# RWKV-7 attention with a hardswish feed-forward: the load of unit 4's r moved behind the second group's preparation, and the second inversion's steps moved behind a stage's results

## The chip, the cores and the metric

The kernel runs on one core of one Trainium2 chip. The metric is the device time of one execution in microseconds (us), the median of several; less is better. Nothing else runs on the chip.

## The reference, cut to what matters

All data are float32. The first half is a recurrence over 768 time steps for 4 batches of 8 heads, each with a 40x40 state; the second is a two-layer feed-forward on its output.

```python
B, H, S, D = 4, 8, 768, 40
for t in range(S):
    y[:, :, t] = einsum('bhd,bhde->bhe', r_t, state)
    Sa = einsum('bhde,bhe->bhd', state, a_t)
    state = state * w_t[:, :, None, :] - einsum('bhd,bhe->bhde', Sa, b_t)
    state = state + einsum('bhd,bhe->bhde', v_t, k_t)
x = y.transpose(0, 2, 1, 3).reshape(3072, 320)
h = x @ w_in                                   # 320 -> 2048
out = (h * clip(h + 3, 0, 6) / 6) @ w_out      # 2048 -> 320
```

## The kernel before, in words

**Units and groups.** Time is cut into blocks of 64 steps. A *unit* is two batches by one such block; there are 24. Four units form a *group* (two blocks of time by two pairs of batches); unit 4 to unit 7 are the second group. Within a block the recurrence is written as matrix products, which need the inverse of a triangular matrix per head.

**Preparation of a unit** (function `prepare`, L582) is a list of stages. Most have two halves: *products* on PE into PSUM, a `yield PE`, and then *results*, which ACT, DVE or POOL take out of PSUM. The stages are W and gam (the decays), A, B, K (PE transposes of the loaded a, b, k at L506, then a product with the decays on DVE: L650, L658, L736), F (the triangular matrix: L672 on PE, L676 on ACT), factor (PE L710, ACT `rgt` L717, then POOL makes the scaled k and b, `KBt`, L725), E (scores at L554 on PE, then the mask, `copy_predicated` L578, on DVE) and EV (PE L752, ACT L757). A stage also issues the loads of a later unit that reuse the buffers it has just read (`fetch`, L490 for w, a, b, k; L487 for v; L478 for r and for a of later units).

**Inversion** (function `invert`, L779) takes the F of a whole group: a transpose on DVE (L784), a copy on ACT (L794), cuts and memsets on POOL (L789, L791, L796), then 30 pairs of a product (L804) and a sum (L810) on DVE, and two transposes at the end (L813, L818). It is a generator. Each call `aside(n)` issues its next n steps; the first step issues everything up to L796, the next two issue nothing, and then each step is one DVE instruction.

**Feed-forward.** `feed_forward` is a generator too; `pieces(n)` issues its next n pieces: 8 matmuls of expand (L1171; results on ACT L1193 and DVE L1194) or 2 or 4 of contract (L1219).

**Order.** Every engine runs its instructions in program order, so the order in which these generators are advanced is the order on each engine. SP issues nearly all DMAs, in program order as well. While the first group's last stages run by a written plan (loop at L1416, lines t = 10 to 15 of it), `by_twos` (L1309) prepares units 4 to 7 beside them: in its line t it runs one stage of units 4 and 5 (t below 9) and one of units 6 and 7 (t = 3 and t above 5), with feed-forward pieces after each. Units 6 and 7 have their F stage in line 10, after which the second inversion is put on the list `side`; lines 11, 12 and 13 are their factor, E and EV stages. What is left of `second_group` is run at L1446, then 18 times three steps and 1.25 pieces (L1448), then the rest of the inversion.

Then the main loop begins with unit 4's own steps: `begun_beside` clears buffers on POOL (L567, L570), `fade` scales the state (L911, L913), and `RT` turns r on DVE (L531). That is the first use of unit 4's r.

The two places that the change touches, L1323 to L1324 and L1431 to L1434:

```python
                    run(chains[i], steps if t > 10 else 0, mixed, 1 if t < 5 else 0)
                pieces(rate / 2)
...
        if t == BEGIN + 2:
            fetch("V", NU)
            fetch("V", NU + 1)
            fetch("R", NU)
```

`run(stage, steps, ...)` calls `aside(steps)` at each `yield PE`, so between a stage's products and its results. `mixed` is 0 in the only call.

Of the kernel before, what the change touches and what calls it, by code (L numbers as in the profile page):

```python
# [31 lines left out]
def kernel(  # L32
# [47 lines left out]
    NU = 2 * NP  # L80
# [30 lines left out]
    def begun_ffn():  # L111

        lent.__exit__(None, None, None)
        pairs.clear()
        pairs.append(("pair", 2))
        pools["h"] = ctx.enter_context(tc.tile_pool(name="hidden", bufs=1, space=PSUM))
# [77 lines left out]
    def second(name):  # L194

        tag = {"B": "S", "K": "U"}[name]
        return padded(grp.tile([P, H, SLOT], F32, name=name + "1", tag=tag, bufs=1), name)

    def seconds():
        t = inv.tile([P, 2, H, SLOT], F32, name="WA1", tag="x", bufs=1)  # L200
        for i, name in enumerate("WA"):
            others[name] = padded(t[:, i], name)
# [28 lines left out]
    for i in range(3):  # L231
        t = area[:, EDGE + i * H * BL:EDGE + (i + 1) * H * BL]
# [14 lines left out]
    for p in range(NP):  # L247
        t = const.tile([P, 2, NPR, SLOT], F32, name=f"state{p}")
        nc.vector.memset(t[:], 0.0)
        state.append(t)  # L250
        t = const.tile([P, 2, NPR], F32, name=f"last{p}")
# [16 lines left out]
    for i, (x, y) in enumerate([(0, DFF // 2), (0, NJ // 2)]):  # L268
        for n, z in enumerate((x, y)):
            t = win[:, :, z:z + H * SLOT] if i == 0 else \  # L270
                wout[:, z:z + 4, :].rearrange("p j m -> p (j m)")[:, 0:2 * H * SLOT].rearrange(
                    "p (n x) -> p n x", n=2)
            t = t.rearrange("p n (h e) -> p n h e", e=SLOT)
# [4 lines left out]
    for u in range(2):  # L278
        t = win2[:, u * NPR * P:(u + 1) * NPR * P]
# [171 lines left out]
    def fetch(name, i, engine=None):  # L451

        if i is None or i >= NK:
            return
        x, crossed = {"W": (w, 0), "A": (a, 0), "B": (b, 0), "K": (k, 0), "R": (r, 1),
                      "V": (v, 1)}[name]
        if name == "V":
            t = values[i % AHEAD]
        else:
            t = placed.get((name, i))  # L460
            if (name, i) == ("R", 1):
                t = others["K"]
            if (name, i) == ("W", NU + 1):
                t = values[NU]
            t = t if t is not None else (others if i < 2 * NU and i % 2 and name != "R" else inputs)[name]
        g, p = names[i]
        engines = engine or nc.sync
        if name == "R" and i >= NU or name == "A" and i >= 2 * NU:
            y = x[2 * p:2 * p + 2, :, g * BL:(g + 1) * BL, :]
            n = 2 if name == "R" else 1  # L470
            y = y.rearrange("q (k s j) t e -> s j (q k) (t e)", s=2, j=n).rearrange(
                "s j k (l e) -> s j l k e", e=2 * D)
            for s in range(2):
                for c in range(0, D, L):
                    z = s * SLOT + c
                    to = rooms[name][z:z + L].rearrange("l (j k e) -> l j k e", j=n, e=2 * D)
                    for j in range(n):
                        nc.sync.dma_start(out=to[:, j, :, 0:2 * D - c], in_=y[s, j, :, :, c:])  # L478
            data[i][name + "N"] = t
            return  # L480
        for q in range(2):
            engine = engines[q] if isinstance(engines, tuple) else engines
            y = x[2 * p + q, :, g * BL:(g + 1) * BL, :]
            rows = slice(q * BL, (q + 1) * BL)
            if crossed:
                for s in range(2):
                    engine.dma_start(out=t[rows, 4 * s:4 * s + 4, 0:D],  # L487
                                     in_=y[s::2].rearrange("h t e -> t h e"))
            else:
                engine.dma_start(out=t[rows, :, 0:D], in_=y.rearrange("h t e -> t h e"))  # L490
        data[i][name + "N"] = t
# [272 lines left out]
    def in_turn(stages, order):  # L764

        for name in order:
            yield from stages[name]()
            shared[0] = None
            yield DONE

    def by_stages(i, stages):


        scanned = [] if i < NU + 2 else ["W", "gam"]
        order = ["K", "factor", "F"] if i % NU < 2 else ["K", "F", "factor"]
        return in_turn(stages, scanned + ["A", "B"] + order + ["E", "EV"])
# [476 lines left out]
    def pieces(n):  # L1253

        owed[0] += n * (8 / 9 if spread[0] else 1)
        while owed[0] >= 1:
            owed[0] -= 1
            if not next(stream):
                owed[0] = 0.0

    def aside(n, weight=0):

        for _ in range(n):
            if side and next(side[0], side) is side:
                side.popleft()
            due[0] += weight
            while due[0] >= 1:
                due[0] -= 1
                next(weights, None)

    def deal(n):

        for _ in range(n):
            next(weights, None)

    def run(stage, steps=0, mixed=0, deals=0):

        for at in stage:
            if at == DONE:
                return  # L1280
            aside(steps, mixed)
            deal(deals)
# [13 lines left out]
    def prepared(i):  # L1296
        nonlocal F
        if i >= NK:
            return None
        if i % NU == 0:  # L1300
            F = lazy_F()
        return prepare(i, F)
# [6 lines left out]
    def by_twos(first, steps, mixed, rate):  # L1309


        chains = [by_stages(first + i, prepared(first + i)) for i in range(NU)]
        for t in range(TWOS):

            order = [0, 1] if t < STAGES else []
            order += [2, 3] if t > 5 else []
            if t < 2:
                order = [0, 1, 0, 1][4 * t:]
            if t == 3:
                order = [2, 0, 3, 1]  # L1320
            for i in order:
                if t >= 2 or first != NU:
                    run(chains[i], steps if t > 10 else 0, mixed, 1 if t < 5 else 0)  # L1323
                pieces(rate / 2)  # L1324
            if t == 10:
                side.append(invert(group_F[-1], third, first == 0))
            yield
# [12 lines left out]
    chains = [in_turn(begin[i], [x[1:] for x in FIRST + BESIDE if x[0] == str(i)]) for i in range(NU)]  # L1340
# [17 lines left out]
    chains = [in_turn(stages[0], ["RT", "VT", "C", "R"]), in_turn(stages[1], ["RT", "VT", "C"])]  # L1358
# [25 lines left out]
    def block(i, j):  # L1384

        if i % NU < 2:
            if j == 0:
# [24 lines left out]
    chains = {str(i): in_turn(stages[i], [x[0][1:] for line in plan for x in line if x[0][0] == str(i)])  # L1412
              for i in range(NU)}
    chains.update({x: firsts[n] for n, x in enumerate("XY")})
    chains.update({x: in_turn(prepare(NU + n, None), ["W", "gam"]) for n, x in enumerate("PQ")})
    for t, line in enumerate(plan):  # L1416
        if t == 8:
            begun_ffn()
            ring.clear()
            ring.extend([("one", 1), ("whole", 2)])  # L1420
        for name, *amounts in line:
            run(chains[name[0]], 0, 0, *map(int, amounts))
        limit[0] = {3: 15, 8: 17, 9: PIECES}.get(t, limit[0])
        if t == BEGIN - 2:
            seconds()
            third.clear()
            second_group = by_twos(NU, 3, 0, 1.25)
        if t == BEGIN:
            fetch("A", NU + 1)
            fetch("W", NU + 3)  # L1430
        if t == BEGIN + 2:  # L1431
            fetch("V", NU)
            fetch("V", NU + 1)
            fetch("R", NU)  # L1434
        if t == BEGIN + 1:

            for name in "BK":
                others[name] = second(name)
                fetch(name, NU + 1)
        if t >= BEGIN - 2:  # L1440
            pieces(3 if t < BEGIN else 1.5 if t < BEGIN + 3 else 0)
        if t >= BEGIN:
            next(second_group)
    for _ in weights:
        pass
    for _ in second_group:  # L1446
        pass
    for _ in range(18):  # L1448
        aside(3)
        pieces(1.25)  # L1450
# [154 lines left out]
```

## Time and profile before

| what | value |
|---|---|
| median of three timed runs | 775.2 us (773.38 to 775.27) |
| the profiled execution | 772.7 us |
| its span, first to last instruction | 771.0 us (1.7 us lie around it) |
| PE, TensorE matmul, busy | 710.8 us (92%) |
| DVE, VectorE, busy | 508.8 us (66%) |
| ACT, ScalarE, busy | 310.4 us (40%) |
| POOL, GpSimd, busy | 150.8 us (20%) |
| mean granted TensorE clock | 0.956 |

In timelines a row reads: start in us from the beginning of the span, length in us, engine, line of the code, operation, what it writes and reads, shape, count; a bracket gives how long the engine was idle before it and what ended the wait. SPq is the queue of SP, where a row is the time that the issue of DMAs took. PEld is the load of a matmul's stationary operand, and PEclk the share of full clock granted to TensorE.

### The profile page before, as it was taken

Reading aid. Unit: us, or ns where it says so; the run is one execution under the profiler, and the core shown is the slowest. Engines: PE = TensorE matmul, PEld = TensorE weight load, DVE = VectorE, ACT = ScalarE, POOL = GpSimd, SP = SyncE. Lnnn points to the kernel's source line nnn. Section 1 sums busy time; section 2 is a strip of 40 time slices with the busy share of each in tenths; the row PEclk is TensorE's granted clock in tenths of the full one; section 3 lists DMA queues with packets and bytes.
Section 4 is the critical chain, followed back from the end, with each engine's and each line's share of the span. In section 5 each row is a group of like instructions: output and inputs, shape, how many; then the busy total and the mean of one; then the engine's idle time right before and its main releaser. Section 6 shows DMA issues by size and latency. Waiting matters only on the chain.

```text
span 771.0 us, 33034 instructions
## 1 busy us (share of the span) xinstructions
PE 710.8 (92%) x14568; PEld 603.1 (78%) x14568; DVE 508.8 (66%) x1027; ACT 310.4 (40%) x644; POOL 150.8 (20%) x303
## 2 busy tenths in 40 slices
PE   4635888999899989999999999999999999999997
PEld 3534777778779778888888888888888888888885
DVE  8899968588557799556798456898436982333210
ACT  2377865232553324552434453234444224322211
POOL 7403210321322211212112121203112010000000
PEclk7956799999999999999999999999999999999999
DMA  9685563420334322233322223313331110110000
GB/s 124 119 179 150 114 170 57 79 43 18 64 65 84 70 55 48 52 71 60 64 52 55 53 62 63 69 37 60 57 72 42 25 24 23 35 35 12 14 16 19
DMA packets 175999, 48.43 MB, mean 63 GB/s; under 512 B 159216, under 2 KB 174576, under 8 KB 175856
## 3 DMA queue, kind: packets, MB, share of 16 engines
q1 hardware_dynamic: 171552, 45.58, 29.7%
q8 instruction: 115, 1.88, 1.0%
q10 hardware_dynamic: 4304, 0.74, 0.7%
q14 instruction: 28, 0.23, 0.1%
HBM read 37.62 MB, written 3.93 MB: 54 GB/s over the span
## 4 chain that ended last, share of the span: by engine, by line
PE 77%; DVE 8%; SPq 5%; issue 3%; DMA 3%; ACT 3%; POOL 0%; DVEq 0%; ACTq 0%; POOLq 0%
PE o L1219 25%; PE h L1171 24%; PE pair L554 4%; PE pair L1064 4%; SPq L490 3%; PE h L1184 2%; PE one L506 2%; PE pair L968 2%; PE pair L927 1%; DVE prod L804 1%; PE pair L1007 1%; PE pair L516 1%; PE pair L752 1%; DVE x L810 1%; PE pair L1023 1%
## 5 line engine op out<-in xcount | busy, mean ns | idle before, releaser
L1171 PE MATMUL h<-xt,win 128*128 128x128 f32 (+1 forms) x2000 | 229.2, 282 | 3.0 <-DVE gt L1194 3.0
L1219 PE MATMUL o<-wout,gt 128*128 128x320 f32 x768 | 230.4, 443 | 0.0
L1171 PEld LDWEIGHTS h<-xt,win 128*128 128x128 f32 (+1 forms) x2000 | 212.9, 193 | 17.5 <-issue 3.1
L1219 PEld LDWEIGHTS o<-wout,gt 128*128 128x128 f32 x768 | 138.6, 190 | 50.3 <-issue 0.2
L1193 ACT ACTIVATE gt<-h,three 128x512 f32<-128x512 f32 x96 | 62.6, 686 | 110.3 <-PE h L1171 88.0
L1194 DVE SCALAR_TENSOR_TENSOR gt<-gt,h 128x512 f32<-128x512 f32 x96 | 61.8, 679 | 62.4 <-ACT gt L1193 62.3
L578 DVE COPY_PREDICATED area<-mask,pair 128x512 f32<-128x512 int32 x56 | 40.5, 726 | 55.2 <-PE pair L554 36.7
L804 DVE TENSOR_TENSOR prod<-x 128x30 f32<-128x30 f32 (+9 forms) x180 | 64.1, 356 | 8.9 <-POOL x L789 3.3
L810 DVE TENSOR_TENSOR x<-x,prod 128x30 f32<-128x30 f32 (+9 forms) x180 | 63.0, 350 | 5.5
L725 POOL TENSOR_TENSOR KBt<-K,rgt 128x320 f32<-128x320 f32 x22 | 19.1, 866 | 142.2 <-ACT rgt L714 134.2
L1071 DVE TENSOR_TENSOR ys<-pair,ys 128x512 f32<-128x512 f32 x20 | 13.8, 690 | 40.5 <-PE pair L1064 40.5
L993 POOL COPY area<-V 128x320 f32<-128x320 f32 x20 | 9.1, 454 | 149.6 <-DVE area L645 53.7
L757 ACT ACTIVATE EV<-pair 64x320 f32<-64x320 f32 x44 | 19.0, 432 | 39.2 <-PE pair L752 38.9
L1064 PE MATMUL pair<-area,KBt 64*64 64x104 f32 x1280 | 32.4, 250 | 0.0
L1237 ACT ACTIVATE ob<-o 128x320 f32<-128x320 f32 x22 | 9.6, 435 | 56.6 <-PE o L1219 35.2
L603 DVE TENSOR_TENSOR_SCAN prods<-area,start 128x528 f32<-128x528 f32 x24 | 29.9, 1250 | 3.4 <-ACT area L599 3.3
L632 POOL COPY gam<-prods 128x256 f32<-128x256 f32 x24 | 12.7, 531 | 99.1 <-DVE prods L603 99.1
L614 DVE TENSOR_TENSOR_SCAN area<-area,start 128x528 f32<-128x528 f32 x24 | 30.6, 1276 | 0.8
L1064 PEld LDWEIGHTS pair<-area,KBt 64*64 64x64 f32 x1280 | 29.9, 133 | 1.5 <-issue 1.4
L872 ACT ACTIVATE tinv<-pair 32x256 f32<-32x256 f32 x48 | 18.0, 375 | 31.9 <-PE pair L862 31.3
L931 DVE TENSOR_TENSOR RR<-pair,EV 128x320 f32<-128x320 f32 x22 | 10.7, 485 | 20.9 <-PE pair L554 13.6
L633 POOL COPY rgam<-prods 128x256 f32<-128x256 f32 x22 | 23.9, 1084 | 0.0
(289 smaller groups left out, 1078.5 us busy)
## 6 DMA issues: line engine op xcount, KB each, us to landing
V<-in_v_dram SPq DMA_DIRECT2D x96, 40.0 KB
out_dram<-ob SPq DMA_DIRECT2D x47, 80.0 KB
R<-in_r_dram SPq DMA_DIRECT2D x92, 40.0 KB
B<-in_b_dram SPq DMA_DIRECT2D x42, 80.0 KB
K<-in_k_dram SPq DMA_DIRECT2D x42, 80.0 KB
W<-in_w_dram SPq DMA_DIRECT2D x37, 80.0 KB
A<-in_a_dram SPq DMA_DIRECT2D x37, 80.0 KB
xt<-yg SPq DMA_DIRECT2D x72, 40.0 KB
```

The lines of the kernel that those rows point to most:

```text
L554: nc.tensor.matmul(out=o[i][half(q), n ^ (2 * q * placed), :], lhsT=lhs[half(i, D), n ^ (2 * q * swap), half(q)], rhs=rhs[half(i, D), n, h ...
L578: nc.vector.copy_predicated(out=x[:].rearrange("p (i h) t -> p i h t", i=2), mask=mask8, data=o[2])
L603: nc.vector.tensor_tensor_scan(out=prods[:].rearrange("p r m i -> p (r m i)"), data0=wm[:, 0:SCAN], data1=start[:], initial=0.0, op0=ALU.m ...
L614: nc.vector.tensor_tensor_scan(out=back, data0=back, data1=start[:], initial=0.0, op0=ALU.mult, op1=ALU.add)
L633: nc.gpsimd.tensor_copy(rv[:, :, 0:HB], o["prods"][:, :, 0, 0:HB][:, :, ::-1])
L804: nc.vector.tensor_tensor(out=pv, in0=_ap(x[:], (i + 1) * L + i, [[L, n], [0, i]]), in1=_ap(x[:], i * L, [[0, n], [1, i]]), op=ALU.mult,)
L810: nc.vector.tensor_tensor(out=rest, in0=rest, in1=pv, op=ALU.add)
L1064: nc.tensor.matmul(out=both[q][half(s), pr, :], lhsT=o[name][half(q), h * D:h * D + SLOT], rhs=beside[name][half(q), 4 * rs + 2 * (s ^ (q ...
L1171: nc.tensor.matmul(out=hp[c][:, i, :], lhsT=lhsT, rhs=rhs, start=(begun[c] == 0), stop=(begun[c] == 3 * NQ - 1))
L1193: nc.scalar.activation(out=gt[:], in_=hp[c][:], func=AF.Relu, bias=three[:], scale=1.0)
L1194: nc.vector.scalar_tensor_tensor(out=gt[:], in0=gt[:], scalar=6.0, in1=hp[c][:], op0=ALU.min, op1=ALU.mult)
L1219: nc.tensor.matmul(out=op[:], lhsT=gts[c][:, n, :], rhs=wout[:, c * HJ + r * NQ + n, :], start=((split or r == 0) and c == 0 and n == 0), ...
```

## The change

```diff
@@ by_twos
             for i in order:
                 if t >= 2 or first != NU:
-                    run(chains[i], steps if t > 10 else 0, mixed, 1 if t < 5 else 0)
+                    run(chains[i], 0, 0, 1 if t < 5 else 0)
                 pieces(rate / 2)
+                aside(steps if t > 10 else 0)
@@ the written plan
         if t == BEGIN + 2:
             fetch("V", NU)
             fetch("V", NU + 1)
-            fetch("R", NU)
...
     for _ in second_group:
         pass
+    fetch("R", NU)
     for _ in range(18):
```

The first hunk: in lines 11 to 13 of the second group's preparation (factor, E and EV of units 6 and 7) three steps of the inversion were issued between a stage's products and its results; now they are issued after the results and the feed-forward pieces that follow. There are 18 such steps before and after. PE's order is the same. On DVE each of the two masks L578 (E of unit 6, E of unit 7) stands three steps earlier among the inversion's steps. On ACT the `rgt` of unit 6 (L717) now stands ahead of the inversion's copy (L794), and on POOL the `KBt` of unit 6 (L725, twice) ahead of the cuts and memsets (L789 to L796).

The second hunk: the eight DMAs that load unit 4's r (L478) move on SP from behind unit 5's v to behind the b and k of unit 8. Between their old and new places SP issues a of units 6 and 7, w of unit 8, the moves of unit 3's result (L1111, L1116), b and k of units 6 and 7, v of units 6 and 7, a of unit 8, and b and k of unit 8.

## The prediction, as put on record

> **What bounds the kernel.** First the page's busy shares: PE is busy 710.8 of 771.0 us and the chain that ended last is PE for 77% of the span. PE's work is not changed, so time can only come from PE's idle, and only where the idle isn't given back before PE is full again. In the table of 10 us stretches PE is full from 210 to 270 us; so I look at what moves the point at which PE becomes full. The change acts from 129.5 us (old place of r's load) to about 192 us (end of the second inversion). I read SP's timeline there first:
>
> ```profile
> 129.51 3.93 SPq L478 DMA_DIRECT2D R<-in_r_dram  x8
> 133.53 1.28 SPq L490 DMA_DIRECT2D A<-in_a_dram  x2
> 134.91 2.01 SPq L490 DMA_DIRECT2D WA<-in_a_dram  x2
> 137.03 1.27 SPq L490 DMA_DIRECT2D W<-in_w_dram  x2
> 138.40 3.09 SPq L1111 DMA_DIRECT2D xt<-yg  x4
> 141.53 2.47 SPq L1116 DMA_DIRECT2D xt<-yg  x4
> 144.12 1.35 SPq L490 DMA_DIRECT2D B<-in_b_dram  x2
> ```
>
> See that each row starts where the one before it ends: SP waits for nothing, its issuing is the limit. The b of unit 6 (last row) and that of unit 7 (issued from 146.94 us on) could have gone earlier, since their buffers were last read by POOL's KBt, which ended at 136.6 and 138.3 us. Then PE's timeline, for who waits:
>
> ```profile
> 148.93 0.63 PE L506 MATMUL one<-ident,B 128*128 128x128 f32 x4 [1.30 <-DMA B<-in_b_dram]
> ...
> 150.93 0.63 PE L506 MATMUL pair<-ident,B 128*128 128x128 f32 x4 [0.48 <-DMA B<-in_b_dram]
> ...
> 163.21 0.68 PE L752 MATMUL pair<-V,area 64*64 64x40 f32 x32 [1.50 <-DVE area L578]
> ...
> 199.84 0.75 PE L862 MATMUL pair<-zs,tt 32*32 32x32 f32 x64 [1.21 <-DVE area L645]
> ```
>
> PE waits twice for that b, once for the mask of E, and once at 199.84 us for DVE, after the inversion. From 163.2 to 198.6 us PE is full, and DVE nearly so. Which one carries the end of this stretch is told by DVE:
>
> ```profile
> 159.55 0.20 DVE L804 TENSOR_TENSOR prod<-x 128x30 f32<-128x30 f32 x1 [0.66 <-POOL x L789]
> ...
> 160.86 0.83 DVE L804 TENSOR_TENSOR prod<-x 128x84 f32<-128x84 f32 x1
> ...
> 162.43 0.72 DVE L578 COPY_PREDICATED area<-mask,pair 128x512 f32<-128x512 int32 x1
> ...
> 172.91 1.28 DVE L1194 SCALAR_TENSOR_TENSOR gt<-gt,h 128x512 f32<-128x512 f32 x2 [0.65 <-ACT gt L1193]
> ```
>
> DVE waits 0.66 us for the inversion's first cut and 0.65 us at 172.91 for PE's expand; from there the chain of waits runs along DVE without a break to the inversion's last transpose, over POOL's clearing and DVE's scans to PE at 199.84. So PE is the limit up to 172 us and **DVE from 172.9 to 199.8 us**. A gain on PE in the first part counts in full; later it counts only as far as DVE follows.
>
> **Part 1, r's load.** Eight issues go: the next row starts at 133.53 instead of 129.51, so 4.02 us. All behind it may move up by that: a of 6 and 7 (last read by PE at 125.9), w of 8 (read until 127.4) and unit 3's moves (their source was written by POOL until 126.9) are free by their new times. The b of unit 6 goes at 140.1 (buffer free 136.6), that of unit 7 at 142.9 (free 138.3). Before, PE started on the first b 4.81 us after its first issue (144.12 to 148.93); so it is there at 144.9, and PE comes to it at 147.5 (end of the L1171 before it): the 1.30 us go. The second was there at 150.9, becomes 146.9, and PE comes at 150.93 - 1.78 = 149.15: the 0.48 us go too. The k's move with them. What is late next: the banks `one` and `pair`, whose readers end at 144.9 (DVE L650) and 147.9 (ACT L757), ahead of PE's new times. Bounds: 1.30 if the second wait stays, 1.78 if both go; I take **1.78**, because the lead of 4.02 is over twice both waits together. F, DVE's transpose and the inversion all follow this PE work, so they move too.
>
> What r loses: its new place is behind the b and k of unit 8, at 163.82 + 1.3 = 165.1 us in old times, and with about 8 us for issue and landing (3.93 us, and 4.8 us as b needed) it is there by 174. Its first reader is L531 at 194.71, some 20 us of cover, so it costs nothing. Without cover each us late would be a us on DVE's chain. The queue behind it is empty until 177.16 (output rows), so nothing queues behind r.
>
> **Part 2, the inversion's steps.** I work in old times, with part 1 taken off later. ACT: unit 6's rgt has its PE input at 157.7, but stood behind the copy that waits for DVE until 158.9; it now runs at 157.7. POOL: unit 6's KBt runs from 158.2 to 159.9 (0.87 each, spaced 0.82) and the first cut only after it:
>
> ```profile
> 159.01 0.50 POOL L789 TENSOR_SCALAR_AFFINE_SELECT x<-fb 128x256 f32<-128x256 f32 x1 [16.89 <-PE pair L710]
> ...
> 160.72 0.87 POOL L725 TENSOR_TENSOR KBt<-K,rgt 128x320 f32<-128x320 f32 x1
> ```
>
> So the cut ends at about 160.35 instead of 159.51: the first L804 starts 0.83 us **later** (160.38). Then three steps of 0.20, 0.21, 0.53 with gaps bring the first mask to 161.4 instead of 162.43: 1.0 us earlier, and PE's wait of 1.50 falls to 0.5. The second mask needs three more steps. Two of them ran 0.83 and (the sum L810 behind it) 0.78 us beside KBt, while the same size alone took 0.25 us (at 185.95 and 186.23); unit 7's KBt now runs from 161.6 to 163.25, so one of them is slow again (0.83), one is not. Second mask: 163.4 instead of 164.50. The next three steps are 0.31 each instead of 0.36, 0.74 and 0.29, and DVE reaches the step that stood at 165.12 at 165.05: **0.07 earlier**, because the later start eats what the fewer clashes give. PE gets 1.0 us more, so expand's results are ready ahead of DVE and the wait of 0.65 at 172.91 goes. Together **0.72**. Bounds: all five clashes gone, 1.95 - 0.83 + 0.65 = 1.8; the late start not repaid at all and the wait kept, -0.8. I take 0.72 since it is built from the nearest rows.
>
> On the clashes, the Trainium skill, "SBUF — State Buffer", on the port pair that DVE and GpSimd share, says that a DVE instruction with two SBUF inputs contends with a GpSimd one that reads SBUF. The trace agrees (0.83 against 0.25 us). By the page alone both of unit 7's clashes stay, and part 2 would be about 0.2 us less.
>
> **Sum.** 1.78 + 0.72 = 2.5 us at 199.8 us; behind that the order is the old one and PE is full from 206 us, so it stays to the end: span 768.5, profiled time 772.7 - 2.5 = 770.2. The profiled execution lies 2.5 below the median of the runs (775.2), so in their terms **772.7**. About 0.3% (2.3 us) is what a measurement of this kernel can tell from no change; the forecast is just beyond it.
>
> **Rivals.** (a) *The clock takes part of it.* The granted clock fell twice after gaps, first here:
>
> ```profile
> 164.00:165.00 1.00, 1.00 (x4) 0.74 0.80 143
> ```
>
> Columns: stretch, its length, PE busy, clock, DMA share and GB/s. It fell after 1.50 us idle and, at 280.5, after 1.91, stayed at 0.5 for 3.4 us, and did not fall after 1.43 (at 121.9) or 1.21 (at 199.8). The first fall goes with part 2's shorter wait; PE then is some 2.7 us ahead at 190 us where DVE is 0.7 ahead (both beyond part 1), and must wait for DVE before L949 (1.5 us) and before L862 (1.9 us). If the clock falls at the second, 3.4 us at half rate cost 1.7: gain 0.8, 774.4. For it: gaps of that size did it. Against: which gap does it depends on where it lies, as 1.43 and 1.50 show. The Trainium skill, "TensorE: Matmul & The Clock Gate", Part 1, says that the clock drops after an idle window of about 3.4 us; by that page neither gap would do it and the forecast stands, but the trace fell at 1.50, so I keep the rival. (b) *Slower.* The same mechanism at both gaps, L949 and L862: two spells, 3.4 us against 2.5, 0.9 slower, 776.1. It decides once both gaps reach 1.5 us. Against it: they are 5 us apart with full-rate contract matmuls between. (c) *The inversion starts late and that isn't repaid*: POOL's order costs 0.8 on DVE, gain 1.78 - 0.8 = 1.0, 774.2. For it: DVE is the limit until 199.8. Against: the clashes are measured. (d) *The load doesn't do what it says*: b's waits were the transfer's, not SP's, and stay; gain 0.7, 774.5. Against: SP's rows have no gap for 30 us.
>
> **How the numbers follow.** Forecast 0.58, (a) 0.17, (b) 0.10, (c) 0.10, (d) 0.05. Within the forecast the gain runs from 2.0 to 3.6 (part 2 at its upper bound with 1.78), mostly beyond 2.3: 0.53 faster and 0.05 within; from the others 0.02 faster, 0.32 within, and 0.08 slower beyond 0.3% (from (b), with the scatter of the runs). So 0.55, 0.37, 0.08. Range: 775.2 - 3.6 = 771.6, less the scatter below the median (1.8, to 773.38) gives 769.8; above, (b) at 776.1. I take 769.7 to 776.2.
>
> **What would show it.** Right: r's issues at about 161 us; b's rows at 140 and 143; no wait for b on PE; the idle before L752 at 0.5 or less; the last transpose of the inversion (187.74) near 185.2, and L862 near 197.3 us. Wrong: a wait for b that stays, L804's first row later than 158.9, a clock of 0.5 between 190 and 205 us, or a wait of DVE at L531 for r.

## The result, and the profile after

| | before | after |
|---|---|---|
| median of 20 timed runs | 774.95 us (772.18 to 777.86) | 772.31 us (770.25 to 776.48) |
| ratio after / before | | 0.9973, 95% interval 0.9961 to 0.9985 |
| the profiled execution, its span | 772.7 us, 771.0 us | 773.5 us, 771.8 us |

The changed kernel takes 2.1 us less by the ratio (1.2 to 3.0; 775 us times one minus the ratio and its ends); the two medians are 2.6 us apart. The forecast was 2.5 us less and 772.7 us. The two profiled executions do not show this by their spans, which are 0.8 us apart the other way; one has to read along the span where they part.

SP's timeline of the changed kernel, from unit 6's a on (start, length, queue, line):

```profile
130.28 1.27 SPq L490 DMA_DIRECT2D A<-in_a_dram  x2
...
140.13 2.16 SPq L490 DMA_DIRECT2D B<-in_b_dram  x2
142.38 1.27 SPq L490 DMA_DIRECT2D K<-in_k_dram  x2
143.76 1.27 SPq L490 DMA_DIRECT2D B<-in_b_dram  x2
...
162.19 4.84 SPq L478 DMA_DIRECT2D R<-in_r_dram  x8
```

Unit 6's a now follows v at once (v ends at 130.18), and the b of units 6 and 7 go at 140.13 and 143.76 instead of 144.12 and 146.94, although PE in this execution was 1.2 us later at the start of the stretch. PE's timeline shows who had waited:

```profile
149.23 0.60 PE L506 MATMUL one<-ident,B 128*128 128x128 f32 x4
149.67 1.06 PE L1171 MATMUL h<-xt,win 128*128 128x128 f32 x8
150.56 0.60 PE L506 MATMUL pair<-ident,B 128*128 128x128 f32 x4
...
161.67 0.68 PE L752 MATMUL pair<-V,area 64*64 64x40 f32 x32 [0.49 <-DVE area L578]
...
193.83 0.63 PE L949 MATMUL one<-ident,state 128*128 128x128 f32 x4 [1.13 <-DVE state L913]
...
198.73 0.75 PE L862 MATMUL pair<-zs,tt 32*32 32x32 f32 x64 [1.51 <-DVE area L645]
```

No bracket for b is left; the wait for the mask is 0.49 instead of 1.50; the wait before L862 is longer than before (1.51, was 1.21), and one before L949 is new. DVE's timeline shows what became of the second part:

```profile
159.96 0.21 DVE L804 TENSOR_TENSOR prod<-x 128x30 f32<-128x30 f32 x1 [1.48 <-POOL x L789]
...
162.10 0.81 DVE L804 TENSOR_TENSOR prod<-x 128x84 f32<-128x84 f32 x1
162.95 0.25 DVE L810 TENSOR_TENSOR x<-x,prod 128x84 f32<-128x84 f32 x1
163.11 0.72 DVE L578 COPY_PREDICATED area<-mask,pair 128x512 f32<-128x512 int32 x1
...
171.78 1.27 DVE L1194 SCALAR_TENSOR_TENSOR gt<-gt,h 128x512 f32<-128x512 f32 x2
```

The inversion's first step waits 1.48 us for POOL's cut instead of 0.66; of the two steps of 84 elements one is still slow, one is not; the wait for expand (0.65 at 172.91 before) is gone. The later start and the fewer clashes cancel: the sum of 130 elements starts 10.77 us behind L672 of units 6 and 7 in both profiles (165.12 before, 164.72 after). All that DVE gained on L672 in this pair came at the wait for expand. And behind L862 the granted clock falls. The columns of a row of stretches are its bounds, its length, PE busy, granted clock, DMA share and GB/s:

```profile
198.00:200.00 2.00, 1.27 (x67) 0.91 0.39 69
200.00:202.00 2.00, 2.00 (x11) 0.50 0.37 60
202.00:204.00 2.00, 2.00 (x27) 0.73 0.40 68
```

Put side by side, the starts of the same instructions tell where the time went and where it came back:

| instruction | before | after | after less before |
|---|---|---|---|
| L1085, the second with its 1.43 us wait (ahead of the change) | 121.94 | 123.16 | +1.22 |
| L752 of units 4 and 5 (ahead of b) | 145.40 | 147.17 | +1.77 |
| L672 of units 6 and 7 (behind b) | 154.35 | 153.95 | -0.40 |
| L862, the first | 199.84 | 198.73 | -1.11 |
| L1023 behind it | 205.60 | 206.12 | +0.52 |
| end of the span | 771.0 | 771.8 | +0.8 |

So in this pair of executions the stretch with b gave 2.17 us (from +1.77 to -0.40), the stretch with the inversion's steps 0.71, and the fall of the clock took 1.63 (L862 to L1023 took 7.39 us instead of 5.76). Of the 1.77 us at the top, 1.22 arose before r's old place and 0.55 in a gap of PE at L672 of units 4 and 5. That gap is not the change's: a second profile of the kernel before, shown below, has one of 0.70 us at the same instruction.

### The profile page after: what moved, and what is told of

Its sections match the earlier page's. It is cut to its first block, busy times and chain, and to the rows that moved or that the text cites. A ratio compares the mean times of both kernels' runs of the same rounds, so it can differ in the third digit from the quotient of the medians.

```text
span 771.8 us, 33032 instructions
## 1 busy us (share of the span) xinstructions
PE 711.8 (92%) x14568; PEld 603.5 (78%) x14568; DVE 507.6 (66%) x1027; ACT 310.6 (40%) x644; POOL 150.1 (19%) x303
## 3 DMA queue, kind: packets, MB, share of 16 engines
HBM read 37.62 MB, written 3.93 MB: 54 GB/s over the span
## 4 chain that ended last, share of the span: by engine, by line
PE 77%; DVE 9%; SPq 5%; issue 3%; DMA 3%; ACT 3%; POOL 1%; DVEq 0%; ACTq 0%; POOLq 0%
PE h L1171 25%; PE o L1219 24%; PE pair L554 4%; PE pair L1064 4%; SPq L490 3%; PE h L1184 2%; PE one L506 2%; DVE prod L804 2%; DVE x L810 2%; PE pair L927 2%; PE pair L968 2%; PE pair L1007 1%; PE pair L516 1%; PE pair L1023 1%; PE one L949 1%
## 5 line engine op out<-in xcount | busy, mean ns | idle before, releaser
L1194 DVE SCALAR_TENSOR_TENSOR gt<-gt,h 128x512 f32<-128x512 f32 x96 | 61.8, 680 | 62.2 <-ACT gt L1193 62.0
L578 DVE COPY_PREDICATED area<-mask,pair 128x512 f32<-128x512 int32 x56 | 40.7, 727 | 56.4 <-PE pair L554 37.9
L804 DVE TENSOR_TENSOR prod<-x 128x30 f32<-128x30 f32 (+9 forms) x180 | 64.1, 356 | 9.7 <-POOL x L789 3.3
L725 POOL TENSOR_TENSOR KBt<-K,rgt 128x320 f32<-128x320 f32 x22 | 19.1, 869 | 158.8 <-ACT rgt L714 135.9
L633 POOL COPY rgam<-prods 128x256 f32<-128x256 f32 x22 | 25.8, 1174 | 0.0
```

The source lines that it names most:

```text
L578: nc.vector.copy_predicated(out=x[:].rearrange("p (i h) t -> p i h t", i=2), mask=mask8, data=o[2])
L633: nc.gpsimd.tensor_copy(rv[:, :, 0:HB], o["prods"][:, :, 0, 0:HB][:, :, ::-1])
L804: nc.vector.tensor_tensor(out=pv, in0=_ap(x[:], (i + 1) * L + i, [[L, n], [0, i]]), in1=_ap(x[:], i * L, [[0, n], [1, i]]), op=ALU.mult,)
L1194: nc.vector.scalar_tensor_tensor(out=gt[:], in0=gt[:], scalar=6.0, in1=hp[c][:], op0=ALU.min, op1=ALU.mult)
```

## The experiments

Two theories stood against each other. Mine: SP's issuing sets when b arrives, r's place brings 1.8 to 2.2 us, the steps' order 0.7. The rivals: r's bytes delayed b; the order of the steps is what counts, or costs; the clock takes the gain.

**1. Each part alone.** Part 1 is the changed kernel with the old order of steps, part 2 the kernel before with the new order:

```diff
 # part 1 alone, against the changed kernel
-                    run(chains[i], 0, 0, 1 if t < 5 else 0)
+                    run(chains[i], steps if t > 10 else 0, mixed, 1 if t < 5 else 0)
                 pieces(rate / 2)
-                aside(steps if t > 10 else 0)
 # part 2 alone, against the kernel before
-                    run(chains[i], steps if t > 10 else 0, mixed, 1 if t < 5 else 0)
+                    run(chains[i], 0, 0, 1 if t < 5 else 0)
                 pieces(rate / 2)
+                aside(steps if t > 10 else 0)
```

> Part 1 alone: r's load moved, the inversion's steps where they were. My theory (SP's issuing set b's arrival): no wait for b on PE, b's rows on SP 4.0 us nearer to v's rows, PE 1.8 to 2.2 us earlier from the second b on; PE's wait for the mask stays at about 1.5 us and DVE's wait for the cut at about 0.7; whole gain 1.8 to 2.2 us, ratio to before 0.9974. Rival 1 (the order of the steps is what brings the time): gain under 0.7, ratio 0.999 or more. Rival 2 (PE's lead is lost at the clock after the inversion): the profile shows the gain at 199 us but a granted clock of 0.5 behind it, gain about 0.5.

Measured: 772.54 us, ratio 0.9981 (0.9965 to 0.9997). No wait for b on PE; the wait for the mask stayed:

```profile
162.61 0.67 PE L752 MATMUL pair<-V,area 64*64 64x40 f32 x32 [1.60 <-DVE area L578]
```

> Part 2 alone: the inversion's steps behind the results, r's load in its old place. My theory: the waits for b stay (1.8 us in all), PE's wait for the mask falls from 1.5 to 0.5, DVE starts the inversion 0.8 us later and is 0.1 earlier after the second mask, its wait for expand at 172.9 goes; gain 0.7 us if the gate of the clock fell in that place before, about 0.1 if it did not; ratio 0.999 to 1.000. Rival 1 (the late start is not repaid): 0.8 us slower, ratio 1.001. Rival 2 (the masks count in full on PE): gain 1.0 to 1.5, ratio 0.998.

Measured: 774.50 us, ratio 0.9999 (0.9987 to 1.0012). The waits on PE changed as expected, one for b being left and that for the mask being short:

```profile
151.98 0.63 PE L506 MATMUL pair<-ident,B 128*128 128x128 f32 x4 [1.58 <-DMA B<-in_b_dram]
...
163.25 0.68 PE L752 MATMUL pair<-V,area 64*64 64x40 f32 x32 [0.48 <-DVE area L578]
```

So part 1 brings the time and part 2 alone brings nothing that 12 runs can tell. Rival 1 of the first text (the order is what counts) is not borne out. Rival 2 of the first text shows in the profile, where the clock fell behind L862, but the time, 1.5 us less (0.2 to 2.7), does not decide how much that costs on average. Rival 1 of the second text, a loss of 0.8 us, is not excluded by the time, whose interval reaches 0.9 us on the slow side; the profiles of experiment 3 put the loss at 0.2 us or less. Rival 2 of the second text, a gain of 1.0 to 1.5 us, would need the far end of the interval (1.0), and the profiles show no such gain.

**2. SP's issuing or r's bytes?** A kernel that issues eight DMAs at r's old place again, each with a quarter of the bytes (one of the four heads that a DMA carries), and the full load at the new place:

```diff
             fetch("V", NU + 1)
+            fetch("R", NU, 1)
...
-    nc.sync.dma_start(out=to[:, j, :, 0:2 * D - c], in_=y[s, j, :, :, c:])
+    nc.sync.dma_start(out=to[:, j, 0:engine or 4 * (3 - n), 0:2 * D - c],
+                      in_=y[s, j, :, 0:engine or 4 * (3 - n), c:])
```

> The changed kernel with eight more DMAs at r's old place, each moving a quarter of what r's load moves there (its full load stays at the new place). This splits SP's issuing from the transfer. My theory (issuing): the eight rows cost SP nearly what they did, 3 to 4 us, b's rows come 3 to 4 us later than in the changed kernel, and PE waits for b again, 1 to 2 us in all; ratio to before 0.999. Rival (the bytes of r delayed b): a quarter of the bytes, so no wait for b, or under 0.5 us, and the ratio stays at 0.997.

Measured: 774.05 us, ratio 1.0001 (0.9982 to 1.0020). SP first, then PE:

```profile
130.70 3.85 SPq L478 DMA_DIRECT2D R<-in_r_dram  x8
...
145.50 1.35 SPq L490 DMA_DIRECT2D B<-in_b_dram  x2
```

```profile
152.11 0.63 PE L506 MATMUL pair<-ident,B 128*128 128x128 f32 x4 [1.15 <-DMA B<-in_b_dram]
```

Eight issues with a quarter of the bytes take SP 3.85 us, against 3.93 with all of them; b is late again, PE waits again, and by its median the gain is gone (its interval, from 0.9982 up, hardly overlaps that of the changed kernel, which ends at 0.9985). The bytes are not what delayed b; the issues ahead of it are.

**3. Which falls of the clock belong to the program?** Both kernels were profiled once more, unchanged.

> The kernel before, profiled once more. Which of its gaps lets the clock fall? My theory (a gap near 1.5 us lets it fall or not, by where it lies): the order and the waits are the same as in the first profile within 0.4 us; the fall at 164 us and that behind L862 may each be there or not; where that at 164 is missing, DVE's wait for expand at 172.9 is missing too. Rival (the falls belong to the program): the fall at 164 is there again and none behind L862.

> The changed kernel, profiled once more. My theory (a gap near 1.5 us lets the clock fall or not, by where it lies): waits as in its first profile within 0.4 us, and the fall behind L862, which cost 1.6 us there, may be missing; then L862 to L1023 takes 5.8 us and not 7.4. Rival (the falls belong to the program): fall and 7.4 us again.

Of the kernel before, the second profile has the same 1.50 us wait of PE, but the clock stays at 1.00 behind it, and DVE's wait at the first L1194 behind the masks is missing. PE, then DVE, then the clock:

```profile
162.84 0.68 PE L752 MATMUL pair<-V,area 64*64 64x40 f32 x32 [1.50 <-DVE area L578]
```

```profile
171.79 1.28 DVE L1194 SCALAR_TENSOR_TENSOR gt<-gt,h 128x512 f32<-128x512 f32 x2
```

```profile
164.00:166.00 2.00, 1.88 (x39) 1.00 0.73 121
166.00:168.00 2.00, 2.00 (x21) 1.00 0.09 18
```

Of the changed kernel, the second profile has the same 1.50 us before L862, and no fall behind it. PE, then the clock:

```profile
197.83 0.75 PE L862 MATMUL pair<-zs,tt 32*32 32x32 f32 x64 [1.50 <-DVE area L645]
```

```profile
200.00:202.00 2.00, 2.00 (x62) 1.00 0.28 46
```

L862 to L1023 takes 203.59 - 197.83 = 5.76 us. One program, the same gap, the fall once and once not: the falls behind gaps of 1.5 us do not belong to the program. With all profiles the price of each part can be read without them:

| kernel | steps' order | L752 to L672 (b between) | L672 to L862 | fall at 164 us | fall behind L862 |
|---|---|---|---|---|---|
| before | old | 8.95 | 45.49 | yes | no |
| before, again | old | 7.90 | 44.72 | no | no |
| part 1 alone | old | 6.79 | 44.70 | no | yes |
| part 2 alone | new | 8.56 | 44.91 | no | yes |
| eight small DMAs | new | 8.12 | 44.94 | no | no |
| after | new | 6.78 | 44.78 | no | yes |
| after, again | new | 6.78 | 44.77 | no | no |

The first column of times is r's part: 6.78 when r is out of the way, 7.90 to 8.95 when it is not. The second is the order's part: 44.71 on average with the old order and 44.77 to 44.94 with the new one, **no gain**, unless the clock fell at 164 us, as it did in the one profile that I had predicted from. What the shorter gap is worth on average stays open: of the three profiles with the old order one has the fall at 164 us, at a price of 0.77 us (45.49 - 44.72); of the nine with another order, those of experiments 4 to 6 among them, none has.

**4. r's cover.** r's load moved further, behind the 18 rounds:

```diff
-    fetch("R", NU)
     for _ in range(18):
         aside(3)
         pieces(1.25)
+    fetch("R", NU)
```

> The changed kernel with r's load moved once more, behind the 18 rounds of inversion steps and pieces; on SP it then stands behind the two pairs of output rows. My theory (r has some 20 us of cover): its rows move from 162 to about 187 to 191 us, it lands at 192 to 193, L531 at 193.6 waits under 0.5 us, and the time is that of the changed kernel, ratio to before 0.997. Rival (r's landing sets L531): L531 waits 1 us or more for r, all of DVE's chain behind it moves by as much, ratio 0.9985 or more.

Measured: 772.16 us, ratio 0.9976 (0.9961 to 0.9990), as the changed kernel. In SP's row the first 8 of the 16 issues are unit 4's, the others unit 5's:

```profile
184.86 10.53 SPq L478 DMA_DIRECT2D R<-in_r_dram  x16
```

```profile
191.29 0.76 DVE L531 STREAM_TRANSPOSE RT<-R 128x256 f32<-128x256 f32 x2
```

r's first reader waits for nothing even now. From r's first issue to its first reader the changed kernel had 31.4 us (162.19 to 193.60), this one has 6.4 (184.86 to 191.29): 25 us of the cover are used up and it costs nothing.

**5. The late start against the clashes.** The factor steps ahead of the results again, E's and EV's behind them:

```diff
-                    run(chains[i], 0, 0, 1 if t < 5 else 0)
+                    run(chains[i], steps if t == 11 else 0, 0, 1 if t < 5 else 0)
                 pieces(rate / 2)
-                aside(steps if t > 10 else 0)
+                aside(steps if t > 11 else 0)
```

> The changed kernel with the steps of line 11 (factor of units 6 and 7) ahead of the results again, those of E and EV behind them. On ACT and POOL the inversion's copy and cuts stand ahead of unit 6's rgt and KBt as before; DVE's order is that of the changed kernel. My theory (late start and clashes cancel): DVE's wait for the first cut falls from 1.48 to about 0.7 us, the first mask comes 0.8 us earlier, but three or four steps beside KBt take 0.5 us more each, so the step behind the second mask is 0.3 us later than in the changed kernel; time equal within 0.5 us. Rival (the late start is what counts): inversion's end 0.7 us earlier, 0.7 us less.

Measured: 771.99 us, ratio 0.9976 (0.9961 to 0.9990). DVE's timeline:

```profile
156.85 0.20 DVE L804 TENSOR_TENSOR prod<-x 128x30 f32<-128x30 f32 x1 [0.67 <-POOL x L789]
...
159.00 0.81 DVE L804 TENSOR_TENSOR prod<-x 128x84 f32<-128x84 f32 x1
159.85 0.83 DVE L810 TENSOR_TENSOR x<-x,prod 128x84 f32<-128x84 f32 x1
```

The start is 0.8 us earlier, three steps run beside KBt (the third, the sum of 58 elements, takes 0.56) where the changed kernel has two, and L672 to L862 is 44.61: 0.17 shorter, where I had expected 0.3 longer. The late start and the clashes nearly cancel, as the theory said, but I had put the balance on the wrong side. In the medians it can't be told.

**6. Can PE's idle behind the inversion be used?** Three kernels bring two feed-forward pieces forward, ahead of L949 and L862, and pay the debt later: the first directly behind L862, the second half a unit after that, the third in unit 5 (this one with the edit of experiment 5 too):

```diff
     for _ in range(18):
         aside(3)
         pieces(1.25)
+    pieces(2)
     aside(3 * L)
...
                 block(i, j)
+            if i == NU and j == 1:         # j == 3; i == NU + 1 and j == 1
+                owed[0] -= 2
```

> The changed kernel with two feed-forward pieces of 8 matmuls brought forward, from behind PE's wait at L862 into PE's idle ahead of it; all else in the old order. My theory (behind the inversion PE runs dry while DVE sets the end, 1.1 us before L949 and 1.5 before L862 in the changed kernel's profile): the pieces fill this idle, both waits fall below 0.7 us, the clock stays at 1.0 there, 1.5 to 2 us less than the changed kernel, 3.0 if the clock's loss goes as well; ratio to before 0.994 to 0.995. Rival (the pieces delay the products that DVE waits for, so the end of DVE's chain moves by as much): same time as the changed kernel, ratio 0.997.

> The changed kernel with two feed-forward pieces brought forward ahead of L949 and L862, like the kernel that filled the idle, but the debt is paid three quarters of a unit later (behind the mask and state stages of unit 4), so that 8 or more dense matmuls stay behind L862. Theory (that kernel lost its gain because the clock fell for two spells in the stretch that it had emptied): no wait before L949, about 1 us before L862, no fall of the clock between 200 and 210 us in most executions, 1.5 to 2.5 us less than the changed kernel, ratio to before 0.9945 to 0.996. Rival (the pieces delay DVE's chain by what they fill): same time as the changed kernel, ratio 0.997.

> The kernel with the factor steps ahead, with two pieces brought forward as well and the debt paid in unit 5's second quarter. Theory: as for the kernel above, and 0.2 us less from the earlier end of the inversion; ratio to before 0.994 to 0.996. Rival (the pieces delay DVE's chain): ratio 0.997 as without them.

Measured: 773.02 us, 0.9976 (0.9954 to 0.9998); 772.64 us, 0.9971 (0.9946 to 0.9995); 775.21 us, 0.9997 (0.9969 to 1.0026). None can be told to be faster than the changed kernel, and the third loses the gain by its median. The wait before L949 went in all three and that before L862 fell only to 1.06, 1.10 and 1.16, since L672 to L862 grew to 45.14, 45.18 and 45.00 us (44.78 without them, 44.61 in the kernel that the third adds them to). The pieces delay the end of DVE's chain, as the rivals had it. In the first the clock then fell for two spells in the stretch from which the pieces had been taken; three of its 12 runs took 768.6 to 769.3 us, the other nine 772.6 to 776.1. That those three are the runs without the fall was not shown, as only one execution is profiled:

```profile
200.00:202.00 2.00, 1.57 (x62) 0.80 0.37 61
202.00:204.00 2.00, 0.91 (x33) 0.50 0.46 85
204.00:206.00 2.00, 2.00 (x66) 0.50 0.56 124
206.00:208.00 2.00, 2.00 (x11) 0.50 0.34 67
```

In the second no fall came there, but PE ran dry 14 us on, where the debt was paid, and there the clock fell instead (0.65 on average from 216 to 218 us, 0.50 from 218 to 220):

```profile
216.01 0.47 PE L516 MATMUL pair<-ident,B 64*128 64x64 f32 x8 [1.96 <-issue]
```

In the third PE ran dry for 1.95 us at 224.79, and the clock then stayed at half for some 10 us (0.72 on average from 226 to 228 us, 0.50 from 228 to 236, 0.72 from 236 to 238). So the idle was moved, with the risk of a fall behind it, but in these three ways it was not used.

## Why the prediction was right, point by point

**What bounds the kernel**: right. PE's idle was the place, and a gain ahead of 172 us reached 199 us: from L672 to L862 part 1 alone takes 44.70 us, the kernel before, again, 44.72.

**Part 1, 1.78 us**: the mechanism was right in each step. SP's gapless rows were the limit; b's rows moved to 140.1 (as forecast) and 143.8 (forecast 142.9; the two issues of unit 6's b took 2.16 us instead of 1.35); both waits went; the inversion moved with them. (PE comes to the first b at 147.6 by the rows, not 147.5; nothing hangs on it.) The size is 1.1 to 2.2 us by the table: it depends on how late PE itself comes to b in an execution, because SP's rows do not move with it. In the second profile of the kernel before PE came 0.7 us later (L752 at 146.10, not 145.40), b was issued 0.46 us earlier, and the first of the two waits was not there at all. Part 1 alone measured 1.5 us (0.2 to 2.7); the forecast lies inside.

**r costs nothing in its new place**: right, shown by experiment 4.

**Part 2, 0.72 us**: this is the term that failed. What the order does to PE and DVE came out nearly as worked out: PE's wait for the mask fell from 1.50 to 0.49 (forecast 0.5), and the late start ate the gain on DVE (forecast 0.07 left; the table says 0.1 to 0.2 lost). One clash more than foreseen stayed: the sum of 58 elements took 0.55 us, 0.22 before. The other 0.65, DVE's wait at 172.91, was real in the profile, but was the price of a fall of the clock which the second profile does not have. I had read a chance event of one execution as a property of the program. Part 2 alone measured 0.1 us (-0.9 to 1.0).

**The clock as a rival**: it happened as described, in the profiled execution itself: PE ran ahead, gaps of 1.13 and 1.51 us opened before L949 and L862 (forecast 1.5 and 1.9), the clock fell behind the second, 1.63 us were lost (forecast 1.7). It was put as a case beside the forecast, and is a chance within each execution: three of the seven profiles of the table have it, two of the kernel before do not. It also comes with part 2 alone and with part 1 alone. That it is likelier in the changed kernel than before is open; the runs' scatter, some 6 us in each kernel, hides a difference of a fraction of 1.6 us.

**The signs that were named.** Two signs of being wrong showed in the first profile: a clock of 0.5 between 190 and 205 us, and L804's first row at 159.96, later than 158.9. The second is the late arrival of this execution; counted from L752 of units 4 and 5 the row came after 12.79 us, 14.15 before. For the same reason the inversion's last transpose (186.60) and L862 (198.73) lie 1.4 us behind the forecast places.

So the sum of 2.5 came near the measured 2.1 with one term right, one absent, and part 1 larger in some executions than the waits in brackets said. That it came so near is in part luck: 1.78 alone lies in the measured interval (1.2 to 3.0) as well, and the runs cannot tell the two.

## What to carry to other kernels

Where a queue's rows follow each other without a gap, count the issues ahead of a transfer that something waits for, not their bytes, and move those that nobody needs soon behind it. Before a wait in one profile is put into a sum, look whether the granted clock fell ahead of it; profile the unchanged kernel a second time, and count only the waits that come again. An order that helps one engine's next wait, but starts the chain of the engine that sets the end later, can give nothing, as here.

## What the runs showed of the hardware

Where the clock fell twice in one execution, the two falls lie a whole number of equal steps apart. From the shares in the stretches (2 us with clock 0.91 are 0.36 us at half speed, so the fall came at 199.64), the changed kernel's falls are at 199.64 and 281.56, those of part 1 alone at 199.68 and 281.60, of part 2 alone at 201.80 and 283.72: 81.92 us apart each time, 24 steps of 3.413. In the kernel before they are at 164.48 and 280.54: 116.06, 34 steps of 3.414. The clock records of all twelve traces agree: each stretch at full or at half clock between two changes lasts a whole number of these steps, from 1 to 197. The program does not keep to the steps: in the three executions with 81.92 us the fall came 0.91, 1.20 and 1.49 us behind the start of L862. This fits a clock that is judged in fixed windows that run on whatever the program does, and it would explain a gap of 1.5 us that lets the clock fall in one execution and not in the next. In the changed kernel's first profile the gap before L862 lies whole between two borders of the steps (196.24 and 199.66 us); in its second a border, at 197.58, cuts it. That is not the whole rule: in the second profile of the kernel before the gap of 1.52 us before L862 lies whole between 195.48 and 198.89, and the clock did not fall. What else decides stays open.

The Trainium skill, "TensorE: Matmul & The Clock Gate", Part 1, gives such a free-running window with 3413 ns, and the runs agree; it has the drop after an idle window, while here gaps of 1.5 us within a busy stretch were enough.

The eight issues took SP 3.93 us with 24 to 40 KB each and 3.85 us with a quarter of that.
